# Routing by quarters, column-grouped logits and longer runs of slot work in an attention and mixture-of-experts kernel

## The chip, the cores and the metric

The kernel runs on one core of one Trainium2 chip. The metric is the device time of one execution in microseconds: before the change the median of 3 runs is 875.09 us (871.43 to 876.87). The profile is of one more execution, recorded by the hardware profiler; its span is 896.0 us. Five engines work side by side: TensorE (PE: matmuls and transposes; PEld is its weight load), VectorE (DVE), ScalarE (ACT), GpSimd (POOL) and SyncE (SP, which issues most transfers).

## The reference, cut to what matters

A sliding-window attention (8 batches, 8 heads, 576 positions, head width 64; four heads with a plain window of 32, four with a dilated one) makes 4608 rows of 512 numbers. Each row goes to one of 8 experts, chosen by the largest of 8 logits, and is multiplied by that expert's two matrices and by a gate.

```python
B, H, S, D = q.shape                      # 8, 8, 576, 64
scores = scale * np.matmul(q, k.transpose(0, 1, 3, 2))
...                                       # masks: window 32, or dilated by 4
attn = np.exp(scores); attn = attn / (np.sum(attn, -1, keepdims=True) + 1e-09)
x = np.matmul(attn, v)                    # then (B,H,S,D) -> (B*S, H*D) = (4608, 512)

logits = x @ w_gate                       # (4608, 8)
expert_idx = np.argmax(logits, axis=1)
probs = np.exp(logits - logits.max(-1, keepdims=True))
probs /= probs.sum(-1, keepdims=True) + 1e-09
gate_w = probs[np.arange(N), expert_idx]
...                                       # rows sorted by expert
h = np.maximum(x_sorted[lo:hi] @ w1[e], 0.0)      # w1[e]: 512 x 1024
y_sorted[lo:hi] = h @ w2[e]                       # w2[e]: 1024 x 512
return gate_w[:, None] * y                        # rows in their old order
```

All data is fp32.

## The kernel before

One Python program emits the instructions of three jobs, and a small clock in it decides how they are interleaved. A scheduler orders them within each engine.

**The attention** goes through 32 units (a batch has four: two kinds of window, two pairs of heads). Each unit turns q and k (`turned`), makes the scores in 64x64 pieces of the array (`scores`), the softmax (DVE, ACT, POOL), turns the weights (`weights`, two units later) and multiplies by v in 64-column pieces (`xo`). Its result is a quarter of `xT`, the batch's rows with the 512 features on the partitions. `yield` hands over to the other jobs with an estimate of cost.

```python
for i in range(len(units) + LAG):                       # LAG = 2
    if i >= LAG:
        eTs = weights(evs.pop(i - LAG))                 # 9 transposes, DVE copies
        yield 0.8, None
    if i < len(units):
        evs[i], dens[i] = front(qT["q"], qT["k"], units[i][1])   # 18 scores matmuls, softmax
    if 0 < i <= len(units):
        norm(evs[i - 1], dens.pop(i - 1))
    yield 1.7, None
    ...                                                 # turn q, turn k: yield 1.0 each
    if i >= LAG:
        for part in range(2):
            summed(eTs, b2, xTs[b2], ty2, hl2, part)    # 8 to 10 xo matmuls, an ACT copy to xT
            ...
            yield 0.9, (b2, xTs.pop(b2)) if last else None
```

**The routing** of a batch starts when all four quarters of its `xT` (128 x 4 x 576) are there. It turns the rows back (`xrow`), makes the logits, finds the expert, ranks the rows within each expert, and writes them to the expert's bucket in DRAM. After batches 1 to 7 it also makes the tables that say which expert and which bucket rows each slot takes.

```python
def route(b, xT):
    rows = []
    for i in range(NT):                                 # 6 tiles of TT = 96 rows
        ps = bank("xrow")
        for c in range(4):
            nc.tensor.transpose(ps[0:TT, 128*c : 128*c+128], xT[:, c, TT*i : TT*i+TT], ident)
        row = pool.tile([TT, ROW], F32, tag="row", name="row", bufs=6)
        (nc.vector.tensor_copy if i % 2 else nc.scalar.copy)(row[:, 0:DM], ps[0:TT])
        rows.append(row)
        yield
    ps = bank("logits")
    lg = ps[0:TT, 0 : NT * E].rearrange("p (t e) -> p t e", e=E)
    for i in range(NT):
        for c in range(4):                              # 24 matmuls, 8 columns wide
            nc.tensor.matmul(lg[:, i], lhsT=xT[:, c, TT*i : TT*i+TT], rhs=wg[:, c],
                             start=c == 0, stop=c == 3)
        ...
    nc.vector.tensor_reduce(out=top, in_=lg, axis=AX, op=OP.max)
    ...                                                 # one-hot of the first maximum, exp
    nc.vector.tensor_copy(before[:, 0], counts)
    for i in range(NT):
        nc.vector.tensor_tensor(out=before[:, i + 1], in0=before[:, i], in1=oh[:, i], op=OP.add)
    nc.vector.tensor_copy(counts, before[:, NT])
    yield
    ...                                                 # rank: 2 matmuls; gate; idx
    for i in range(NT):
        nc.vector.tensor_copy(rows[i][:, DM : DM + 1], gate[:, i : i + 1])
        nc.vector.tensor_scalar(rows[i][:, DM + 1 : ROW], const("tok", TT)[:, i : i + 1],
                                float(b * S), None, op0=OP.add)
        to_bucket(idx[:, i : i + 1], rows[i], b)        # indirect DMA from POOL's queue
    ...                                                 # yield; tables(s): some 30 small DVE operations
```

**The slots** are the experts' matmuls. A slot takes 128 rows of one expert: four transposes (`xt`), 32 matmuls with w1 (`ph`, in groups of four), and 8 with w2 of 512 columns (`py`). Each group of four `ph`, each `py` and each group of transposes is one piece of the slot generator. Only slots whose rows are already in the buckets may run during the attention (2, 6, 11, 15, 20 and 24 slots after batches 1 to 6). 39 slots run in all.

**The clock** owes slot work in proportion to attention work, and pays it at once, two times an attention step:

```python
ATT, BEHIND = 36.0, 16.0
def run_slots():
    while clock["owed"] > 0:
        while ready and ready[0][0] <= clock["all"]:
            _, upto, over = ready.pop(0)
            clock["upto"] = upto
            clock["rate"] = (SLOT * upto - clock["moe"]) / over
        ...                                             # stop at the last slot that is ready
        c = next(slots)                                 # one piece
        ...
        clock["owed"] -= c

for cost, ended in attention():
    clock["all"] += cost
    clock["owed"] += cost * clock["rate"] / 2 + 1e-6
    run_slots()
    if ended:
        routing.append((ended[0], route(*ended)))
    run_routing()                                       # one step of a routing
    clock["owed"] += cost * clock["rate"] / 2
    run_slots()
```

PSUM has 8 banks, which all matmul results take in turn (`bank`).

Of the kernel before, what the change touches and what calls it, by code (L numbers as in the profile page):

```python
# [29 lines left out]
ROW = DM + 2  # L30
# [14 lines left out]
def _constants():  # L45
# [10 lines left out]
    def mask(ty):  # L56
# [15 lines left out]
        "edge": np.tile(128 * np.arange(N // 128 + 1), (128, 1)),  # L72
# [23 lines left out]
def kernel(  # L96
# [17 lines left out]
    psum = ctx.enter_context(tc.tile_pool(name="psum", bufs=8, space=PSUM))  # L114
# [3 lines left out]
    wg = cpool.tile([128, 4, E], F32, name="wg")  # L118
    nc.scalar.dma_start(wg, moe_w_gate.rearrange("(c p) e -> p c e", p=128))
    counts = cpool.tile([96, E], F32, name="counts")  # L120
    nc.vector.memset(counts, 0.0)
# [201 lines left out]
    def summed(eTs, b, xT, ty, hl, part):  # L323
# [16 lines left out]
        if ty == 0:  # L340
# [5 lines left out]
            nc.scalar.copy(xT[:, hl, 64 * j0 : 64 * j1], xo[:, 0:n])  # L346
        else:
            for j in range(4):
# [5 lines left out]
                xT[:, 2 + hl].rearrange("p (t m a) -> p a m t", m=2, a=2)[:, part],  # L354
# [3 lines left out]
    def attention():  # L358
# [7 lines left out]
        xTs, evs, dens = {}, {}, {}  # L366
        for i in range(len(units) + LAG):
            if i >= LAG:
                eTs = weights(evs.pop(i - LAG))
                yield 0.8, None  # L370
# [4 lines left out]
            yield 1.7, None  # L375
# [8 lines left out]
            if i >= LAG:  # L384
                b2, ty2, hl2 = units[i - LAG]
                if (ty2, hl2) == (0, 0):
                    xTs[b2] = pool.tile([128, 4, S], F32, tag="xT", name=f"xT_{b2}")
                for part in range(2):
                    summed(eTs, b2, xTs[b2], ty2, hl2, part)
                    if part == 1 and hl2 == 1 and b2 + 1 < B:  # L390
                        load_v(b2 + 1, ty2)
                    last = (ty2, hl2, part) == (1, 1, 1)
                    yield 0.9, (b2, xTs.pop(b2)) if last else None

    def route(b, xT):


        rows = []
        for i in range(NT):
            ps = bank("xrow")  # L400
            for c in range(4):
                nc.tensor.transpose(  # L402
                    ps[0:TT, 128 * c : 128 * c + 128], xT[:, c, TT * i : TT * i + TT], ident
                )
            row = pool.tile([TT, ROW], F32, tag="row", name="row", bufs=6)
            (nc.vector.tensor_copy if i % 2 else nc.scalar.copy)(row[:, 0:DM], ps[0:TT])
            rows.append(row)
            yield
        ps = bank("logits")
        lg = ps[0:TT, 0 : NT * E].rearrange("p (t e) -> p t e", e=E)  # L410
        for i in range(NT):
            for c in range(4):
                nc.tensor.matmul(  # L413
                    lg[:, i],
                    lhsT=xT[:, c, TT * i : TT * i + TT],
                    rhs=wg[:, c],
                    start=c == 0,
                    stop=c == 3,
                )
            if i == 2:  # L420
                yield
# [12 lines left out]
        top, best = small("top", NT), small("best", NT)  # L434
        oh, dl, gate = small("oh", NT, E), small("dl", NT, E), small("gate", NT)
        nc.vector.tensor_reduce(out=top, in_=lg, axis=AX, op=OP.max)
        nc.vector.tensor_tensor(out=dl, in0=lg, in1=wide(top), op=OP.subtract)

        nc.vector.tensor_scalar(oh, dl, 0.0, None, op0=OP.is_ge)
        nc.vector.tensor_tensor(out=oh, in0=oh, in1=rev, op=OP.mult)  # L440
# [6 lines left out]
        before = small("before", NT + 1, E)  # L447
        nc.vector.tensor_copy(before[:, 0], counts)
        for i in range(NT):
            nc.vector.tensor_tensor(out=before[:, i + 1], in0=before[:, i], in1=oh[:, i], op=OP.add)  # L450
        nc.vector.tensor_copy(counts, before[:, NT])
# [398 lines left out]
```

## Time and profile before

| | busy us | share of the span | instructions |
|---|---|---|---|
| PE (matmul records) | 820.0 | 92% | 7006 |
| PEld (weight loads) | 633.1 | 71% | 7006 |
| DVE | 327.4 | 37% | 1057 |
| ACT | 204.7 | 23% | 751 |
| POOL | 143.3 | 16% | 131 |

The page cuts the span into 40 slices of 22.4 us; a digit is the busy share of a slice in tenths. PEclk is the granted TensorE clock in tenths of full speed. The table of groups names line, engine, operation, output<-inputs, shape and count, then the busy time, the mean ns of one, and the idle time before them with what ended it. An fp32 matmul appears as two records, a transpose as one. Matmuls are pipelined, so the mean of one is its latency; what it costs the queue is seen from start to start in the timeline.

### The profile page before, as it was taken

Reading aid. Unit: us, or ns where it says so; the run is one execution under the profiler, and the core shown is the slowest. Engines: PE = TensorE matmul, PEld = TensorE weight load, DVE = VectorE, ACT = ScalarE, POOL = GpSimd, SP = SyncE. Lnnn points to the kernel's source line nnn. Section 1 sums busy time; section 2 is a strip of 40 time slices with the busy share of each in tenths; the row PEclk is TensorE's granted clock in tenths of the full one; section 3 lists DMA queues with packets and bytes.
Section 4 is the critical chain, followed back from the end, with each engine's and each line's share of the span. In section 5 each row is a group of like instructions: output and inputs, shape, how many; then the busy total and the mean of one; then the engine's idle time right before and its main releaser. Section 6 shows DMA issues by size and latency. Waiting matters only on the chain.

```text
span 896.0 us, 18185 instructions
## 1 busy us (share of the span) xinstructions
PE 820.0 (92%) x7006; PEld 633.1 (71%) x7006; DVE 327.4 (37%) x1057; ACT 204.7 (23%) x751; POOL 143.3 (16%) x131
## 2 busy tenths in 40 slices
PE   4796978799999999999999989979999999999991
PEld 3685857677777777777777867847777676867770
DVE  4776667654643373344533441231010001101010
ACT  2562526143133222222223212100001010100000
POOL 0213132311311131113111120060000000000000
PEclk9896859889999999999999999989999999999996
DMA  9964638997999769988236546779931291549574
GB/s 196 179 149 111 132 85 305 261 249 232 326 263 309 256 180 263 293 254 284 69 118 190 189 152 228 270 233 336 322 120 48 85 308 59 209 143 322 211 250 179
DMA packets 145578, 187.46 MB, mean 209 GB/s; under 512 B 72206, under 2 KB 86030, under 8 KB 145488
## 3 DMA queue, kind: packets, MB, share of 16 engines
q1 hardware_dynamic: 137984, 165.74, 61.2%
q0 software_dynamic: 6832, 19.71, 6.3%
q8 instruction: 58, 0.95, 0.5%
q10 hardware_dynamic: 672, 0.79, 0.3%
q14 instruction: 32, 0.26, 0.1%
HBM read 216.58 MB, written 22.07 MB: 266 GB/s over the span
## 4 chain that ended last, share of the span: by engine, by line
PE 46%; issue 38%; DVE 5%; POOL 4%; DMA 2%; SPq 1%; another core or an unknown queue 1%; ACT 1%; POOLq 0%; DVEq 0%
PE ph L707 13%; PE py L731 13%; PE xo L332 4%; PE scores L269 3%; PE logits L413 3%; PE weights L317 3%; POOL out_dram L740 2%; PE xrow L402 2%; PE turned L242 2%; PE turned L234 1%; DMA k<-in_k_dram 1%; POOL bucket L157 1%; DVE e L280 1%; DMA w<-in_moe_w_dram 1%; DVE lo L289 1%
## 5 line engine op out<-in xcount | busy, mean ns | idle before, releaser
L707 PE MATMUL ph<-xt,w 128*128 128x128 f32 x2496 | 308.0, 277 | 6.3 <-issue 5.5
L707 PEld LDWEIGHTS ph<-xt,w 128*128 128x128 f32 x2496 | 293.5, 192 | 24.1 <-issue 20.9
L731 PE MATMUL py<-w,h 128*128 128x512 f32 x624 | 293.6, 608 | 6.7 <-DVE h L725 6.7
L731 PEld LDWEIGHTS py<-w,h 128*128 128x128 f32 x624 | 112.3, 193 | 112.5 <-issue 102.3
L292 ACT ACTIVATE e<-e,lo 128x96 f32<-128x96 f32 x288 | 103.6, 362 | 81.2 <-DVE lo L289 73.2
L740 POOL DMA_INDIRECT out_dram<-y,to x39 | 38.5, 986 | 401.5 <-ACT y L735 375.9
L683 DVE COPY xt<-xt 128x512 f32<-128x512 f32 x40 | 27.6, 689 | 191.9 <-PE xt L681 191.8
L307 POOL TENSOR_TENSOR e<-e,rec 128x864 f32<-128x864 f32 x32 | 52.2, 1631 | 236.7 <-DVE rec L306 147.7
L735 ACT ACTIVATE y<-py,x 128x512 f32<-128x512 f32 x39 | 26.7, 686 | 258.1 <-PE py L731 155.8
L319 DVE COPY eT<-weights 96x384 f32<-96x384 f32 x96 | 47.8, 546 | 90.1 <-PE weights L317 83.2
L725 DVE TENSOR_SCALAR h<-ph 128x512 f32<-128x512 f32 x39 | 26.9, 691 | 98.4 <-PE ph L707 86.6
L332 PEld LDWEIGHTS xo<-eT,v 96*64 96x64 f32 x1216 | 44.9, 149 | 22.4 <-issue 16.5
L157 POOL DMA_INDIRECT bucket<-row,idx x48 | 44.7, 930 | 95.1 <-DVE idx L481 31.0
L280 DVE SCALAR_TENSOR_TENSOR e<-scores,cst 128x384 f32<-128x384 f32 (+1 forms) x128 | 47.0, 399 | 27.8 <-PE scores L269 23.4
L332 PE MATMUL xo<-eT,v 96*64 96x64 f32 (+1 forms) x1216 | 52.7, 237 | 4.4 <-issue 4.4
L292 ACT ACTIVATION_READ_ACCUMULATOR e<-e,lo 128x1 f32 x288 | 53.9, 187 | 0.0
L317 PE MATMUL weights<-cst,e 128*96 128x128 f32 x288 | 44.2, 306 | 7.3 <-POOL e L307 6.4
L269 PE MATMUL scores<-kT,qT 64*64 64x96 f32 x1152 | 43.1, 284 | 8.1 <-DVE kT L239 4.5
L269 PEld LDWEIGHTS scores<-kT,qT 64*64 64x64 f32 x1152 | 35.2, 159 | 20.4 <-issue 9.9
L317 PEld LDWEIGHTS weights<-cst,e 128*96 128x96 f32 x288 | 36.7, 143 | 13.2 <-POOL e L307 8.2
L717 ACT ACTIVATE h<-ph 128x512 f32<-128x512 f32 x39 | 23.2, 596 | 97.9 <-PE ph L707 97.3
L353 ACT COPY xT<-xo 128x288 f32<-128x288 f32 x32 | 21.3, 680 | 82.0 <-PE xo L332 71.4
(103 smaller groups left out, 530.9 us busy)
## 6 DMA issues: line engine op xcount, KB each, us to landing
w<-in_moe_w_dram SPq DMA_DIRECT2D x82, 2048.0 KB
x<-bucket SPq DMA_DIRECT2D x41, 257.0 KB
v<-in_v_dram SPq DMA_DIRECT2D x32, 192.0 KB
q<-in_q_dram SPq DMA_DIRECT2D x32, 144.0 KB
k<-in_k_dram SPq DMA_DIRECT2D x32, 144.0 KB
v<-in_v_dram SPq DMA_DIRECT2D x48, 96.0 KB
q<-in_q_dram SPq DMA_DIRECT2D x8, 576.0 KB
k<-in_k_dram SPq DMA_DIRECT2D x8, 576.0 KB
```

What stands on the lines that cost most here:

```text
L157: nc.gpsimd.indirect_dma_start(out=bucket, out_offset=bass.IndirectOffsetOnAxis(ap=idx, axis=0), in_=rows, in_offset=None, bounds_check=NR ...
L269: nc.tensor.matmul(sc[r][64 * c : 64 * c + 64, 96 * (i % 5) : 96 * (i % 5) + 96], lhsT=qT[rows, 64 * j : 64 * j + 64], rhs=kT[rows, first_ ...
L280: nc.vector.scalar_tensor_tensor(out=e[p0:p1, i : i + n].rearrange("p i k -> p (i k)"), in0=sc[r][p0:p1, cols], scalar=-SCALE, in1=const(f ...
L292: nc.scalar.activation(out=e[:, n], in_=e[:, n], func=AF.Exp, bias=lo[:, n : n + 1], scale=-1.0, accum_out=den[:, n : n + 1],)
L307: nc.gpsimd.tensor_tensor(out=e, in0=e, in1=rec.unsqueeze(2).broadcast_to([128, 9, 96]), op=OP.mult)
L317: nc.tensor.transpose(tp[0:96, 128 * i : 128 * i + 128], e[:, a + i], ident)
L319: nc.vector.tensor_copy(eT, tp[0:96, 0:384])
L332: nc.tensor.matmul(xo[DH * h : DH * h + DH, at0 : at0 + nq], lhsT=vt[:, 2 * hl + r, j, :] if ty == 0 else vt[:, hl, j, DH * r : DH * r + D ...
L683: nc.vector.tensor_copy(xt, ps)
L707: nc.tensor.matmul(ph[:, fi], lhsT=w1[:, c, 128 * f : 128 * f + 128], rhs=xt[:, c], start=c == 0, stop=c == 3,)
L731: nc.tensor.matmul(py, lhsT=h[:, f], rhs=w2[:, f], start=f == 0, stop=f == 7)
L740: i = nc.gpsimd.indirect_dma_start(out=out, out_offset=bass.IndirectOffsetOnAxis(ap=to, axis=0), in_=y, in_offset=None, bounds_check=N - 1 ...
```

## The change

It is meant to make the routing cheaper and less of a lump, and to leave the slots' matmuls in longer runs.

1. After each attention unit, its quarter of `xT` (now a tile of its own, 128 x 576) is turned into rows at once, and its share of the logits is added up in a PSUM bank kept for that. The logits are computed the other way round: the gate's weights, padded to 32 columns, are the stationary operand and 192 rows of `xT` the moving one, three of them side by side in three column groups. Two transposes per batch (`lg`) turn the logits back. The rotating banks are 7.
2. The rows of a batch are one tile; the row number is written by one POOL operation, the gate by the reciprocal itself, and the counters are kept in one long tile.
3. The count of blocks in the tables is made with a shift in place of a comparison with a list; the tables are made in eight portions.
4. Slot work is paid only when at least 3.5 is owed (some four pieces).

```diff
-    psum = ctx.enter_context(tc.tile_pool(name="psum", bufs=8, space=PSUM))
+    psum = ctx.enter_context(tc.tile_pool(name="psum", bufs=7, space=PSUM))
+    lpsum = ctx.enter_context(tc.tile_pool(name="lpsum", bufs=1, space=PSUM))
...
+            if i > LAG:
+                b2, ty2, hl2 = units[i - LAG - 1]
+                row_part(b2, 2 * ty2 + hl2, xT)
+                yield 0.9, b2 if (ty2, hl2) == (1, 1) else None
...
+    def row_part(b, c, xT):
+        if c == 0:
+            rows[b] = pool.tile([TT, NT, ROW], F32, tag="rows", name=f"rows_{b}")
+            logits[b] = lpsum.tile([96, 2 * TT], F32, tag="logits", name=f"logits_{b}")
+            nc.gpsimd.tensor_scalar(
+                rows[b][:, :, DM + 1], const("tok", TT), float(b * S), None, op0=OP.add)
+        for i in range(0, NT, 3):
+            ps = bank("xrow")
+            for n in range(3):
+                nc.tensor.transpose(ps[0:TT, 128*n : 128*n+128],
+                                    xT[:, TT*(i+n) : TT*(i+n)+TT], ident)
+            (nc.scalar.copy, nc.vector.tensor_copy)[i // 3](
+                rows[b][:, i : i + 3, 128 * c : 128 * c + 128],
+                ps[0:TT, 0:384].rearrange("p (t d) -> p t d", t=3))
+        for j in range(3):
+            nc.tensor.matmul(logits[b][32*j : 32*j+32], lhsT=wg[:, c],
+                             rhs=xT[:, 2*TT*j : 2*TT*j+2*TT], start=c == 0, stop=c == 3)
+
+    def route(b):
+        row = rows.pop(b)
+        lgs = pool.tile([96, 2 * TT], F32, tag="lgs", name="lgs", bufs=1)
+        nc.vector.tensor_copy(lgs, logits.pop(b))
+        ps = bank("lg")
+        for i in range(2):
+            nc.tensor.transpose(ps[0:TT, 96*i : 96*i+96], lgs[:, TT*i : TT*i+TT],
+                                ident[0:96, 0:96])
...
-        nc.vector.tensor_scalar(oh, dl, 0.0, None, op0=OP.is_ge)
-        nc.vector.tensor_tensor(out=oh, in0=oh, in1=rev, op=OP.mult)
+        nc.vector.scalar_tensor_tensor(
+            out=oh, in0=dl, scalar=0.0, in1=rev, op0=OP.is_ge, op1=OP.mult)
...
-        nc.vector.tensor_copy(before[:, 0], counts)
-        nc.vector.tensor_copy(counts, before[:, NT])
...
-        nc.vector.reciprocal(gate, gate)
+        nc.vector.reciprocal(row[:, :, DM], gate)
...
-            nc.vector.tensor_copy(rows[i][:, DM : DM + 1], gate[:, i : i + 1])
-            nc.vector.tensor_scalar(rows[i][:, DM + 1 : ROW], ...)
-            to_bucket(idx[:, i : i + 1], rows[i], b)
+            to_bucket(idx[:, i : i + 1], row[:, i], b)
...
-        nc.vector.tensor_tensor(out=over, ...  op=OP.is_gt if last else OP.is_ge)
-        nc.vector.tensor_reduce(out=ns, in_=over, axis=AX, op=OP.add)
+        nc.vector.tensor_scalar(cnti, tot[0:p], 127.0 if last else 0.0, None, op0=OP.add)
+        nc.vector.tensor_scalar(nsi, cnti, 7, None, op0=OP.logical_shift_right)
+        nc.vector.tensor_copy(ns, nsi)
...                                           # and seven more yields inside tables(s)
-    ATT, BEHIND = 36.0, 16.0
+    ATT, BEHIND = 32.0, 12.0
+    GRAIN = 3.5
...
+        if clock["owed"] < GRAIN:
+            return
         while clock["owed"] > 0:
```

The costs that the attention reports to the clock are adjusted too (1.1 for 0.8 and 1.7, 0.75 for 0.9).

## The prediction

> **What bounds the kernel now.** I read the page's slices first, then the busy time by stage, then the groups by line, and last the instruction order of one stretch. The slices say which engine is full, and when:
>
> ```profile
> PE   4796978799999999999999989979999999999991
> DVE  4776667654643373344533441231010001101010
> PEclk9896859889999999999999999989999999999996
> ```
>
> From slice 9 on TensorE has no idle tenth except around slices 24 to 26, and its clock is full. Before that (about 25 to 185 us) no engine is full: TensorE shows 6 to 9 tenths at a lowered clock and VectorE 6 to 7. The stage table puts numbers on it (columns: stretch and its length, busy us of PE, PEld, DVE, ACT, POOL, granted clock, DMA share, GB/s):
>
> ```profile
> 25.00:185.00 160.00, 130.85 (x1719) 113.13 (x1718) 113.50 (x373) 67.50 (x306) 41.46 (x33) 0.79 0.70 176
> 185.00:520.00 335.00, 330.96 (x3094) 255.18 (x3093) 149.52 (x487) 95.74 (x361) 61.56 (x54) 1.00 0.76 231
> 520.00:605.00 85.00, 76.08 (x517) 57.26 (x517) 25.78 (x109) 10.21 (x17) 20.00 (x21) 0.94 0.65 225
> 605.00:880.00 275.00, 272.38 (x1577) 199.33 (x1575) 28.05 (x55) 24.40 (x38) 18.47 (x19) 1.00 0.58 203
> ```
>
> So there are three regimes: an attention-only start in which PE and DVE wait for each other, a PE-bound mix (185 to 520), and a PE-bound tail of bare slots (605 to 880, 14.45 us a slot). In the last two, a microsecond taken off PE's queue is a microsecond of the span; nothing else counts there. Hence the question is what PE's queue costs, group by group:
>
> ```profile
> L413 PE MATMUL logits<-wg,xT 128*96 128x8 f32 x384 | 35.3, 230 | 0.0
> L402 PE MATMUL xrow<-cst,xT 128*96 128x128 f32 x192 | 30.6, 279 | 0.8 <-ACT xT L353 0.6
> L269 PE MATMUL scores<-kT,qT 64*64 64x96 f32 x1152 | 43.1, 284 | 8.1 <-DVE kT L239 4.5 <-issue 2.5 <-DVE base L608 0.6
> L332 PE MATMUL xo<-eT,v 96*64 96x64 f32 x1088 | 49.8, 240 | 3.5 <-issue 3.5
> ```
>
> A busy mean (230 ns for an 8-column matmul) is latency, not spacing. The spacing is read from the timeline of PE, by subtracting start times (columns: start, busy, engine, line, group):
>
> ```profile
> 289.98 1.06 PE L707 MATMUL ph<-xt,w 128*128 128x128 f32 x8
> 290.96 1.04 PE L269 MATMUL scores<-kT,qT 64*64 64x96 f32 x36
> 291.94 2.05 PE L707 MATMUL ph<-xt,w 128*128 128x128 f32 x16
> 293.82 0.60 PE L402 MATMUL xrow<-cst,xT 128*96 128x128 f32 x4
> 294.26 1.06 PE L707 MATMUL ph<-xt,w 128*128 128x128 f32 x8
> 295.15 1.02 PE L731 MATMUL py<-w,h 128*128 128x512 f32 x2
> ...
> 306.27 1.95 PE L707 MATMUL ph<-xt,w 128*128 128x128 f32 x16
> 308.15 0.69 PE L332 MATMUL xo<-eT,v 96*64 96x64 f32 x16
> 308.77 1.16 PE L707 MATMUL ph<-xt,w 128*128 128x128 f32 x8
> 309.76 2.13 PE L413 MATMUL logits<-wg,xT 128*96 128x8 f32 x24
> 311.75 0.63 PE L681 MATMUL xt<-cst,x 128*128 128x128 f32 x4
> ```
>
> Each fp32 matmul is two records, a transpose one. Undisturbed, 8 ph records take 295.15 - 294.26 = 0.89 us, 0.111 each; an xrow transpose is (294.26 - 293.82) / 4 = 0.11. Going from ph to xrow and back costs nothing. A visit to the packed array does: 289.98 to 293.82 is 3.84 us for 24 ph (2.67) and one scores group, so the visit is 1.17 us, although its 36 records, in sets of four that run together, need 9 x 0.083 = 0.75. The fixed toll is about 0.42 us a visit. The same sum for xo (306.27 to 309.76 = 3.49, less 24 ph = 2.67, leaves 0.82 for 16 records) gives, with the 20-record visits that take 0.11 longer (so about 0.026 a record), a toll of about 0.40. The old logits are 1.99 us for 24 records, 0.083 each, though only 8 columns wide.
>
> **What the Trainium skill says.** "TensorE: Matmul & The Clock Gate", Part 3 (Packing small matmuls), says matmuls on different 32-column groups run concurrently, with 2.38 times for three groups at 512 columns. This trace agrees in kind: 36 scores records of 96 columns in 0.75 us are four-fold overlap. "TensorEngine Tiling (Array Packing)", Key Properties, says that a change of tiling mode drains TensorE; the 0.4 us toll above is what this trace shows of it. The first page's Part 1 says the clock is halved when PE idles and returns after sustained work; the granted 0.79 of 25 to 185 us against 1.00 later agrees.
>
> **The change part by part.**
>
> 1. Logits. Removed: 384 records x 0.083 = 31.7 us of PE (plus about 0.08 us on each of 16 returns, 1.3). Added: 96 matmuls, 192 records of 192 columns, in 32 visits of six. From 128 columns in 0.111 us and 512 in 0.43 (four py groups' starts), 192 columns should need 0.165 (estimate). Three column groups together, two passes: 0.33 us. But each visit now pays a mode toll that the old, full-height logits did not; I take 0.42 as for scores. In the built order a few visits are split, 35 in all: 35 x 0.42 + 32 x 0.33 = 25.3. The transposes back (16 of 96 columns at 0.083, some 0.4 more for transitions) add 1.7. Sum: 33.0 - 25.3 - 1.7 = 6 us saved. The packing is a smaller gain than it looks, since over half of it goes into tolls.
>
> 2. Slot runs of at least four pieces. Counted in the built orders, runs of slot work fall from 157 to 71, but going in and out of transposes costs nothing, as shown. What counts is that the two halves of one xo are parted less often: xo visits fall from 53 to 47, scores stay at 32. 6 x 0.40 = 2.4 us, and some 20 saved re-entries from the 72- and 96-row q/k transposes at about 0.03 (read from the timeline in the same way), 0.6. Sum: 3 us. The name of the change promises more than this.
>
> 3. VectorE. Removed per batch: 12 one-column writes (48 at 142 and 140 ns over the run: 11.4 us), two counter copies (2.0 + 1.3), one of the two one-hot operations (about 1.5), and most of the 288-wide count of blocks (3.0 + 2.6 + 0.9, for three small operations). Added: a 96x192 copy (about 0.35) and row copies of 96x384 in place of 96x512 (32 x 0.55 against 24 x 0.68, +1.2). Net some 15 us of 327. After 185 us VectorE is at 45% and this is worth nothing. In the start it is about 2 us a batch for three batches, beside PE's share already counted in 1. ScalarE's copies stay equal.
>
> 4. Spread tables and rows. The old routing stood in one lump at a batch's end; now each unit does a quarter, and the tables come in eight portions. In the start this fills PE more evenly. Against it: the logits copy, lg, eleven small VectorE operations and rank now follow closely in PE's queue, and in the first three batches no slot work lies between. I expect up to 2.5 us of PE waiting at lg and 2 at rank per batch, where the old order lost 2.7, 3.5 and 1.3 us before rank. I book parts 3 and 4 together as -2 us, +-6.
>
> 5. Banks. Seven rotating PSUM banks instead of eight, and bursts of three attention steps without slot work between: an evacuation that was hidden can now show. I book +0 to +3 us, say +0.5.
>
> 6. The slot schedule's figures (32 and 12 for 36 and 16) move slots forward by half a slot to one slot against the attention; in a PE-bound stretch this only reorders. Slot 24 is the first that needs the last table; in the new order the table is emitted at slot 22, so it does not starve.
>
> Sum: -6 - 3 - 2 + 0.5 = -10.5, about 1.2%: 875 - 10.5 = 864.5, and I say 864.
>
> **The rivals.** (a) The three column groups do not overlap, because both passes of one matmul hold the queue. Then a visit is 0.42 + 0.99 = 1.41 us, 32 of them 45 us, and the logits cost 12 us more than now: about 882. Against it stands the overlap of scores, and of xo, whose 16 records of 64 columns take 0.42 us, about half of what they would need one after the other. (b) The start is bound by VectorE and the cold clock, and the lighter, evenly spread routing lifts both: with 160 us at 0.79 clock, 10% there is 16 us more, about 850. For it: 113.5 us of VectorE in 160, and eight cold stretches. Against it: the longer lg-rank sequence opens new PE gaps at exactly this place, each of which can cool the clock. (c) The bursts expose VectorE and bank waits in 185 to 520, where now 4 us of 335 are idle. Two microseconds for each of the 17 units there would be 34 us; half a microsecond eats the whole gain: about 873. For it: scores waits for a kT copy only 2.2 us of PE work earlier. Against it: slot work still separates most such pairs, and VectorE is less than half busy. (d) The tail's stall (589 to 597 us, PE waiting for h while the last table is made) could go or grow with the yields: -7 to +5 us.
>
> **Range and chances.** The sure part is small, 6 to 9 us; the start and the tail each scatter by as much. Eight in ten: 850 to 877. Faster by over 2% needs 857.6 or less, that is rival (b) or (d) in its good form: 0.27. Slower by over 2% (892.6) needs (a) and (c) together: 0.05. Within 2%: 0.68.
>
> **What would show it.** Logits groups on PE: start to start of the next group under 0.75 us, and the first full-array matmuls after it spaced wider, prove part 1; 1.2 us or more prove rival (a). PE's gaps over 1 us before lg and rank in the first three batches measure part 4; the busy share of 185 to 520 and waits on DVE there, rival (c); the granted clock of 25 to 185 and the end of the first slot (193.9 us now), rival (b). I am wrong in kind if the first slot ends more than 10 us earlier or later, or if the mixed stretch shows over 10 us of new idle time.

## The result, and the profile after

The changed kernel takes 849.46 us (median of 4 runs, 846.83 to 856.43); the kernel before, run beside it, 875.98 us (4 runs, 871.43 to 881.16). The ratio is 0.9708, with an interval of 0.9626 to 0.979: some 26 us less, where I had booked 10.5. That lies just under my range of 850 to 877, in the case to which I gave a chance of 0.27. The profiled run of the changed kernel is the fastest of the four, with a span of 845.1 us. Absolute times differ by over 3% from chip to chip (the last experiment shows it), so below only ratios to the kernel before in the same comparison are set against each other.

The slices of the changed kernel's page (21.1 us each; rows as before):

```profile
PE   4779797999999999999999999999999999999991
DVE  3788795645533453445333631421010101111110
PEclk9997797999999999999999999999999999999996
```

The reader is to see two things. Before the last slice the clock row has no 5 and no 6 any more, and it shows 9 from the eighth slice (148 us) on instead of the tenth (202 us); and VectorE's row is fuller in slices 3 to 6 (8, 8, 7, 9). The stage table answers to the one in the prediction (same stretches, same columns):

```profile
25.00:185.00 160.00, 137.09 (x1873) 111.51 (x1872) 120.09 (x360) 76.16 (x344) 45.55 (x39) 0.87 0.80 204
185.00:520.00 335.00, 332.78 (x3030) 250.07 (x3029) 142.97 (x445) 90.80 (x336) 63.62 (x59) 1.00 0.76 241
```

In these first 160 us TensorE now issues 1873 records instead of 1719 (although the logits of a batch are now half as many records), at a clock of 0.87 instead of 0.79. The mixed stretch is full, as it was: 332.8 of 335 us. The page's busy shares would not have told this: PE is "93%" busy in the kernel before as it ran again (first experiment) and in the changed one. The Trainium skill, page "Perfetto Trace Analysis", section "Identifying the Most-Contended Engine", calls matmul busy time a bad measure of how near a kernel is to its bound, because matmuls are pipelined; this pair of traces agrees.

So I counted differently. Each PE record gets the start-to-start spacing that it has undisturbed at full clock (ph 0.112 us, py 0.429, transposes of 128 columns 0.109, xo 0.026, scores 0.021, old logits 0.083, all read from these timelines; new logits 0.055, a third of the 0.165 that the prediction estimates for 192 columns). Their sum is PE's work. Elapsed time less the work done by then is what was lost to waits, half clock and mode tolls. In us, from the profiled runs of the kernel before (first experiment below) and of the changed one:

```
                        work   lost by 100   by 200   by 500   by 650   span
before                 739.4          56.7     94.7    114.0    117.3   875.5
changed                719.6          54.5     82.9    104.7    106.5   845.1
```

The difference of 30.4 us is 19.8 less work (the logits, 31.7 -> 10.6, plus 1.3 for `lg`), about 12 less lost before 200 us, and about 1 more lost after it. What is lost after 200 us includes the new tolls. It is more than the 26 us of the medians, since the shortest of four executions stands here against a single one of the kernel before. Both the work and the start are larger than I had them.

### The profile page after: what moved, and what is told of

The parts are those of the page before. It is cut to its first block, busy times and chain, and to the rows that moved or that the text cites. A ratio compares the mean times of both kernels' runs of the same rounds, so it can differ in the third digit from the quotient of the medians.

```text
span 845.1 us, 17762 instructions
## 1 busy us (share of the span) xinstructions
PE 787.1 (93%) x6830; PEld 595.2 (70%) x6830; DVE 314.8 (37%) x955; ACT 203.5 (24%) x759; POOL 145.2 (17%) x139
## 4 chain that ended last, share of the span: by engine, by line
PE 48%; issue 30%; DMA 7%; DVE 7%; POOL 3%; ACT 2%; SPq 1%; POOLq 0%; DVEq 0%; ACTq 0%
PE ph L735 15%; PE py L759 15%; PE xo L335 4%; DMA v<-in_v_dram 4%; PE weights L320 3%; PE scores L272 3%; PE xrow L414 2%; DMA x<-bucket 2%; POOL out_dram L768 2%; ACT e L295 2%; DVE e L283 1%; PE turned L237 1%; PE logits L424 1%; DVE lo L292 1%; PE turned L245 1%
## 5 line engine op out<-in xcount | busy, mean ns | idle before, releaser
L735 PEld LDWEIGHTS ph<-xt,w 128*128 128x128 f32 x2496 | 291.9, 193 | 19.8 <-issue 16.1
L735 PE MATMUL ph<-xt,w 128*128 128x128 f32 x2496 | 300.6, 277 | 0.8 <-DVE xt L711 0.8
L759 PE MATMUL py<-w,h 128*128 128x512 f32 x624 | 280.6, 596 | 0.0
L160 POOL DMA_INDIRECT bucket<-rows,idx x48 | 44.5, 928 | 40.8 <-DVE idx L513 21.1
L335 PEld LDWEIGHTS xo<-eT,v 96*64 96x64 f32 x1216 | 42.3, 145 | 11.5 <-issue 7.5
L335 PE MATMUL xo<-eT,v 96*64 96x64 f32 (+1 forms) x1216 | 48.6, 233 | 1.8 <-DMA v<-in_v_dram 1.7
L320 PEld LDWEIGHTS weights<-cst,e 128*96 128x96 f32 x288 | 33.7, 137 | 9.7 <-POOL e L310 4.7
L272 PEld LDWEIGHTS scores<-kT,qT 64*64 64x64 f32 x1152 | 31.2, 148 | 11.9 <-issue 4.3
L272 PE MATMUL scores<-kT,qT 64*64 64x96 f32 x1152 | 37.7, 269 | 2.0 <-DVE kT L242 1.7
L414 PE MATMUL xrow<-cst,xT 128*96 128x128 f32 x192 | 28.4, 284 | 8.1 <-ACT xT L356 6.9
```

What stands on the lines that cost most here:

```text
L160: nc.gpsimd.indirect_dma_start(out=bucket, out_offset=bass.IndirectOffsetOnAxis(ap=idx, axis=0), in_=rows, in_offset=None, bounds_check=NR ...
L272: nc.tensor.matmul(sc[r][64 * c : 64 * c + 64, 96 * (i % 5) : 96 * (i % 5) + 96], lhsT=qT[rows, 64 * j : 64 * j + 64], rhs=kT[rows, first_ ...
L320: nc.tensor.transpose(tp[0:96, 128 * i : 128 * i + 128], e[:, a + i], ident)
L335: nc.tensor.matmul(xo[DH * h : DH * h + DH, at0 : at0 + nq], lhsT=vt[:, 2 * hl + r, j, :] if ty == 0 else vt[:, hl, j, DH * r : DH * r + D ...
L414: nc.tensor.transpose(ps[0:TT, 128 * n : 128 * n + 128], xT[:, TT * (i + n) : TT * (i + n) + TT], ident,)
L735: nc.tensor.matmul(ph[:, fi], lhsT=w1[:, c, 128 * f : 128 * f + 128], rhs=xt[:, c], start=c == 0, stop=c == 3,)
```

## The experiments

Medians in us; "before" is the kernel before on the same chip in the same comparison. e7, e9 and e10 ran on a second chip, e11 on a third, and the others on one.

| label | what it is | median (runs) | before (runs) | ratio and interval |
|---|---|---|---|---|
| e0_before_again | kernel before | 877.32 (1) | 875.70 (27) | |
| e1_grain_only | before + longer slot runs | 880.84 (22) | 875.70 (27) | 1.006 [1.0037, 1.0083] |
| e2_no_grain | changed, slot work paid at once | 849.95 (7) | 875.70 (27) | 0.970 [0.9672, 0.9729] |
| e3_old_logits | changed, old logits in quarters | 854.03 (6) | 875.70 (27) | 0.9754 [0.9725, 0.9782] |
| e4_light_dve | before + lighter VectorE work | 870.59 (8) | 877.37 (13) | 0.9937 [0.9903, 0.997] |
| e5_lump | changed, rows and logits in a lump | 848.89 (6) | 877.37 (13) | 0.9682 [0.9651, 0.9713] |
| e6_tables_whole | changed, tables in one portion | 856.68 (6) | 877.37 (13) | 0.9687 [0.9631, 0.9743] |
| e7_old_pace | changed, old figures of the schedule | 852.36 (6) | 875.75 (27) | 0.9757 [0.9716, 0.9797] |
| e8_warm2 | changed + filler matmuls in the start | 849.08 (6) | 877.37 (13) | 0.9674 [0.964, 0.9708] |
| e9_lump_old_logits | e5 and e3 together | 855.92 (6) | 875.75 (27) | 0.981 [0.9765, 0.9854] |
| e10_warm_before | before + filler matmuls in the start | 875.53 (22) | 875.75 (27) | 1.0008 [0.9985, 1.003] |
| e11_after_again | changed, on another chip | 882.12 (6) | 904.74 (11) | 0.976 [0.9714, 0.9805] |

No experiment leaves out any of the computation; the results of the filler matmuls in e8 and e10 go unused.

**The kernel before, once more.** The span of the first profile, 896.0 us, lies well above the median of 875, so I took another of the unchanged kernel.

> The kernel before, unchanged, for a second profile. Its first profile was of an execution 2.5% longer than the median. If the stalls of that profile (PE waiting 7 us at 589 us, three gaps of 1.3 us at 519 us, the first slot ending at 193.9 us) belong to the program, they stand here again and the span is near 896 us; if they belong to that one execution, the span is near 876 us and they are gone. The first slot's end then tells how much of the gain of the change lies in the start: theory 'start' (evenly spread routing lets the attention-only stretch run faster) expects the first slot to end at least 12 us later here than the 170.5 us of the changed kernel; theory 'queue' (PE's queue got shorter in the mixed stretch) expects under 6 us.

Its span is 875.5 us. The windows of this run (columns: stretch, length, busy us of PE, PEld, DVE, ACT, POOL, clock, DMA share, GB/s):

```profile
25.00:150.00 125.00, 103.57 (x1414) 92.65 (x1413) 91.97 (x285) 57.36 (x257) 32.46 (x25) 0.73 0.61 148
150.00:200.00 50.00, 44.58 (x494) 36.48 (x493) 31.08 (x111) 18.70 (x82) 12.90 (x11) 0.90 1.01 276
200.00:500.00 300.00, 298.66 (x2778) 232.40 (x2776) 133.44 (x425) 82.28 (x304) 52.08 (x46) 1.00 0.77 240
500.00:830.00 330.00, 330.00 (x2068) 243.50 (x2068) 56.31 (x199) 36.62 (x72) 42.09 (x43) 1.00 0.58 207
```

The same of the changed kernel:

```profile
25.00:150.00 125.00, 102.09 (x1480) 83.68 (x1482) 99.00 (x311) 61.85 (x281) 39.57 (x34) 0.84 0.77 197
150.00:200.00 50.00, 50.00 (x552) 38.55 (x547) 25.88 (x60) 18.22 (x76) 7.80 (x7) 0.99 0.95 264
200.00:500.00 300.00, 297.78 (x2720) 224.05 (x2719) 134.04 (x427) 83.87 (x320) 60.74 (x56) 1.00 0.75 235
```

The stall of the tail (76.08 of 85 us busy in 520 to 605 in the first profile) is not there: 330.00 of 330. My rival (d) was built on it. Whether it came from that one execution or from the chip it ran on isn't known; e11's profile has a stall of its own at 579 to 588 us. This trace is the "before" of what follows. The comparison also shows where the change works: up to 200 us. Up to 150 us PE is busy as long as before (103.6 and 102.1 us), with 66 records more, and VectorE is busier, not less: 99.0 of 125 us instead of 92.0. But the attention is no further by then: both have issued the scores of 15 units, and the loss as counted above is about 80 and 78 us. What differs is the first slot, whose matmuls begin at 132.5 us instead of 146.2, and with slot work at hand PE is busy 50.0 of the next 50 us at a clock of 0.99, instead of 44.6 at 0.90. About 10 of the 12 us come from there.

**Longer slot runs alone, and none.** In the kernel before I put the GRAIN rule alone (157 runs of slot work become 69, xo visits 53 -> 46); in the changed one I took it out (141 runs, 55 xo visits).

```diff
 e1, in the kernel before:            e2, in the changed kernel:
+    GRAIN = 3.5                     -    GRAIN = 3.5
+    if clock["owed"] < GRAIN:       -    if clock["owed"] < GRAIN:
+        return                      -        return
```

> The kernel before with only the rule that slot work is paid from 3.5 owed on. Slot runs fall from 157 to 69, xo visits from 53 to 46. My sum books 7 x 0.40 = 2.8 us plus 0.6 for q/k transposes: 872 to 873 us. A rival in which the runs themselves matter (each switch costs PE something that the start-to-start times do not show) expects 10 us or more: 866 or less. A rival in which bursts of attention expose evacuations expects 878 or more.

> The changed kernel with slot work paid at once as before (141 slot runs, 55 xo visits). By my sum it loses 8 x 0.40 + 0.6 = 4 us against the changed kernel: 853. If the gain is in the longer runs: 865 or more. If it is in the routing by quarters, in the start above all, 850 to 853.

Alone, the longer runs cost 0.6%. Without them the changed kernel keeps its ratio, 0.970. The saved visits are there in the order, but nothing of them reaches the time. In e1's profile 6 us more than in e0 are lost by 550 us (123.4 against 117.0), with 24 us more at half clock. It isn't rival (c), attention steps that wait for each other, for PE waits no more than in e0. From 200 to 550 us, e1 and then e0:

```profile
200.00:550.00 350.00, 349.15 (x3169) 272.11 (x3168) 148.88 (x504) 93.95 (x345) 62.77 (x55) 0.97 0.73 229
200.00:550.00 350.00, 348.66 (x3186) 268.71 (x3185) 150.49 (x503) 93.66 (x336) 62.38 (x56) 1.00 0.73 232
```

PE is as busy, but 20 us of this stretch are at half clock, and none in e0. Why the clock falls there stays open. The change's last-named part is the one that brings nothing.

**The old logits within the new routing.**

```diff
-        for j in range(3):
-            nc.tensor.matmul(logits[b][32*j : 32*j+32], lhsT=wg[:, c],
-                             rhs=xT[:, 2*TT*j : 2*TT*j+2*TT], ...)
+        for i in range(NT):
+            nc.tensor.matmul(logits[b][:, E*i : E*i+E], lhsT=xT[:, TT*i : TT*i+TT],
+                             rhs=wg[:, c, 0:E], ...)
```

The copy `lgs` and the transposes `lg` go as well.

> The changed kernel with the logits of each quarter as before: 96 rows of xT as the stationary operand, 8 columns moving, six tiles a quarter, and no transposing back; everything else as changed. By my sum PE's queue is 6 us longer in all: 855 to 856. If the packed logits cost as much as they save (toll of 0.42 us a visit and more), 849 to 851. If the packing is what brought the gain: 862 or more.

The ratio is 0.9754 instead of 0.9708, with intervals that overlap; against the variants of the changed kernel on the same chip that keep the packed logits and have tighter intervals (e2, e5 and e8; 0.970, 0.968 and 0.967) it is 0.5 to 0.8% slower. The changed kernel's own second ratio (e11, 0.976, on another chip) is no better than e3's, so the size of this gain stays rough. What a packed visit costs is seen in the changed kernel's timeline of PE (start, busy, engine, line, group):

```profile
304.74 1.95 PE L735 MATMUL ph<-xt,w 128*128 128x128 f32 x16
306.53 0.82 PE L414 MATMUL xrow<-cst,xT 128*96 128x128 f32 x6
307.28 0.53 PE L424 MATMUL logits<-xT,wg 128*32 128x192 f32 x6
307.74 0.71 PE L237 MATMUL turned<-cst,q 96*128 96x96 f32 x6
308.29 1.98 PE L735 MATMUL ph<-xt,w 128*128 128x128 f32 x16
310.10 3.60 PE L759 MATMUL py<-w,h 128*128 128x512 f32 x8
```

and in the tile's own view for that stretch (durations in ns, then first and last start):

```profile
L424 PE MATMUL logits<-xT,wg x6: 326/338/351, 307.3 to 307.5; 128*32 128x192 f32 x6
```

All six records start within 0.2 us and each lasts 0.34: three groups run at once, in two passes. From 306.53 to 310.10 there are 3.57 us. Take off 16 ph (1.79), six xrow (0.65) and six `turned` (0.50): 0.63 remain, of which 0.33 is the two passes. The toll is 0.30 us here, if the two passes take the estimated 0.33. The same count over the 11 undisturbed visits of six records between 200 and 520 us gives 0.27 to 0.28 where `turned` follows at once and 0.31 to 0.38 where slot matmuls or transposes follow, against 0.40 to 0.42 for the scores visits of the same kernel. All groups of the logits in the changed kernel (from the groups by form: line, engine, operation, tiles, shape, count, busy us, mean ns, idle before and its cause):

```profile
L414 PE MATMUL xrow<-cst,xT 128*96 128x128 f32 x192 | 28.4, 284 | 8.1 <-ACT xT L356 6.9 <-ACT xT L349 1.2
L424 PE MATMUL logits<-xT,wg 128*32 128x192 f32 x192 | 18.8, 346 | 0.8 <-ACT xT L356 0.8
L440 PE MATMUL lg<-cst,lgs 96*96 96x96 f32 x16 | 2.9, 266 | 3.8 <-DVE lgs L437 3.8
```

Given back by the packing: 3.8 us of waiting for the copy `lgs`, over 16 transposes. The 8.1 us before xrow belong to the quarters, not to the packing: the rows now follow directly on the copy of their quarter.

**VectorE's lighter work alone, in the kernel before.** One tile of rows, the row number by POOL, the reciprocal written into the row, a long counter tile, the merged one-hot, the shift. PE's instructions stay as they are, and their order but for four short moves.

```diff
-            nc.vector.tensor_copy(rows[i][:, DM : DM + 1], gate[:, i : i + 1])
-            nc.vector.tensor_scalar(rows[i][:, DM + 1 : ROW], ...)
+        nc.vector.reciprocal(row[:, :, DM], gate)
+        nc.gpsimd.tensor_scalar(row[:, :, DM + 1], const("tok", TT), float(b * S), ...)
...
-        nc.vector.tensor_copy(before[:, 0], counts)
-        nc.vector.tensor_copy(counts, before[:, NT])
...
```

> The kernel before with only the lighter small operations: one rows tile with the row number written by POOL and the gate by the reciprocal, the long counter tile, the merged one-hot operation, the count of blocks by a shift. Logits, the lump at the batch's end, the pace and the 8 banks stay as before. My sum put this at about 2 us a batch in the first three batches, 6 us at most: 870 to 874. If VectorE bounds the start and this lightening is where the gain is: 862 or less. If the start is set by something else: 874 to 877.

0.9937, which is 5.5 us, and in the profiles the loss up to 200 us falls by 6.5 (94.7 -> 88.2), and no further after. It is an effect of the start alone. Its window shows that it needs no emptier VectorE:

```profile
25.00:150.00 125.00, 104.63 (x1446) 93.82 (x1445) 90.92 (x258) 60.31 (x272) 32.98 (x27) 0.75 0.64 162
```

VectorE is as busy (90.9 us) with 27 instructions fewer, and PE is 32 records further at 150 us. I read this so: in this stretch VectorE's time is a supply, and what is taken off it is spent on the next unit. No run shows that step by itself.

**The lump.** The rows and logits of all four quarters are made at the batch's end again, one quarter a step; everything else stays as changed. This needs 8 tiles for xT and leaves one for the rows.

```diff
-                row_part(b2, 2 * ty2 + hl2, xT)
+                xTs.setdefault(b2, []).append(xT)
...
     def route(b):
+        for c, xT in enumerate(quarters.pop(b)):
+            row_part(b, c, xT)
+            yield
```

> The changed kernel with the quarters' rows and logits done together at the end of the batch, one quarter per step of the routing, as the lump stood before; packed logits, small operations, pace and runs as changed (the quarters wait in eight buffers, the rows have one). If the even spread is what shortens the start, 862 to 870, with the clock of 25 to 150 us falling back towards 0.73. If the spread is worth nothing, 849 to 853.

0.9682: no slower at all. I had expected a loss, so the even spread over the batch, the change's first-named part, isn't where the gain comes from. In its profile the loss by 200 us is 5 us above the changed kernel's, and some 2 us of that come back later; the medians show nothing of it.

**The tables in one portion.**

```diff
-                yield from tables(s)
+                for _ in tables(s):
+                    pass
```

> The changed kernel with the tables made in one portion as before. The slots become ready about one unit earlier by the clock of the program, so slot work starts about half a unit earlier; against it stand some 20 VectorE operations in one stretch. If the eight portions matter: 853 or more. If an earlier first slot is worth more: 846 or less. My sum has it at 849 +-2.

The six runs lie at 845.1, 854.7, 854.8 and three times at 858.6 to 859.0 us; the ratio of 0.9687 [0.9631, 0.9743] leaves out the last three, which count as slow, while the median in the table has all six. With them the result would fall in my "853 or more". No difference can be resolved in either direction.

**Filler matmuls in the changed kernel's start.** To see whether the clock itself limits the start, two constant matmuls of 480 columns per unit run until slots are due, about 20 us of PE's time.

```diff
+    def warm(n):
+        if clock["rate"] == 0.0:
+            for _ in range(n):
+                nc.tensor.matmul(bank("warm")[:, 0:480], lhsT=ident,
+                                 rhs=const("mask0"), start=True, stop=True)
```

> The changed kernel with two matmuls of 480 columns on constants added after each unit's scores and after each unit's logits, only until the first slots are due; their results are not used. They add about 0.8 us of PE each, 25 in all, some 20 us of PE work at full clock. If the half-speed stretches of the start (41 us of the changed kernel's first 151) cost time, and PE waits there anyway, the clock of 25 to 150 us rises from 0.84 to 0.95 or more and the time falls to 840 to 846. If the start is bound by VectorE and waits, and the clock does not matter, the time is 849 to 855. If the added work itself delays: 858 or more.

The clock of 25 to 150 us rises from 0.84 to 0.90 only (I had said 0.95), the time at half clock before 150 us falls from 40 to 27 us, and the ratio is 0.9674: some 20 us of filler neither lengthen nor shorten the time. What the same clock would do without the filler's own time on PE, no run shows.

**The old figures of the slot schedule.**

```diff
-    ATT, BEHIND = 32.0, 12.0
+    ATT, BEHIND = 36.0, 16.0
```

> The changed kernel with the schedule figures of before (36 and 16 for 32 and 12). Slots then stand about half to one slot later against the attention, 18 instead of 19 done when the last batch is routed. I booked nothing for this: 848 to 851. If moving slots forward fills PE's waits of the start, and part of the gain comes from it: 855 or more.

0.9757: about 4 us more than the changed kernel's first ratio, but the intervals overlap, and the changed kernel's second ratio (e11, 0.976) is the same as this one. So a cost isn't shown. In the profile the loss up to 200 us is 88.2 instead of 82.9. PE waits 5.0 us for a transfer of v at 139 us, where the changed kernel's longest such wait is 1.7, and by 150 us 15 us more have passed at half clock. Whether the old figures bring this wait isn't known: e3, with the new ones, has one of 4.0 us at 149 us. I had booked nothing for it.

**Lump and old logits together.** It has the work of the kernel before on PE (739.4 us), with neither the packing nor the spread.

> The changed kernel with both undone at once: the quarters in one lump at the batch's end, and the logits as before. Alone the lump cost nothing and the old logits 4.6 us. If the two parts simply add up, 853 to 855, and the clock of 25 to 150 us stays near 0.84. If the clock falls only where a lump and the thin old logits come together (some 4 us of 8-column matmuls and 2.6 us of transposes in a row, in which the array does little), the clock falls to about 0.75, over 60 us of the first 150 are at half speed, and the time is 861 or more.

0.981 [0.9765, 0.9854], against 0.9682 [0.9651, 0.9713] for the lump with the packed logits: here the packing is worth 1.3%, some 11 us, though the two ran on different chips. The clock of 0.81 and the 55 us of half clock before 150 us lie between my two cases, the median nearer to the additive one. Against e3 the intervals overlap. And it is still 1.9% under the kernel before, with neither of the change's first two names in it. The first stretch of e9, then e5, then e3:

```profile
25.00:150.00 125.00, 109.15 (x1584) 98.87 (x1582) 98.18 (x285) 61.66 (x276) 34.61 (x28) 0.81 0.73 191
```
```profile
25.00:150.00 125.00, 102.39 (x1513) 85.91 (x1511) 98.55 (x299) 64.53 (x293) 34.61 (x29) 0.86 0.75 189
```
```profile
25.00:150.00 125.00, 108.14 (x1490) 97.98 (x1488) 94.77 (x280) 61.37 (x278) 34.64 (x28) 0.84 0.68 180
```

All three have VectorE at 95 to 99 us of 125, above the 92 of the kernel before, whatever the form of the logits. What they share is the rest of the change. But it is no firm mark of the change: the changed kernel's second profile (e11) has 91.7.

**Filler matmuls in the kernel before.** This is the other half of the question about the clock: the same constant matmul, 24 times (48 records), in the start of the unchanged kernel.

> The kernel before with 24 matmuls of 480 columns on constants, until the first slots are due: one after each unit's scores, one after every second tile of rows, two in the logits; their results are not used. They add some 20 us of PE work at full clock. If the 75 us of half clock in the first 150 are what makes the start of the kernel before slow, the clock of 25 to 150 us rises from 0.73 to 0.85 or more and the time falls to 862 to 870 although there is more work. If the clock only follows from waits and costs nothing itself, the time is 874 to 880; if the added work delays, 882 or more.

```profile
25.00:150.00 125.00, 111.80 (x1526) 89.52 (x1525) 93.32 (x294) 61.00 (x276) 34.12 (x26) 0.91 0.64 170
150.00:200.00 50.00, 47.70 (x539) 37.27 (x539) 32.39 (x116) 17.30 (x74) 11.50 (x10) 1.00 0.91 238
200.00:225.00 25.00, 20.59 (x188) 19.43 (x189) 5.95 (x19) 4.42 (x16) 2.66 (x2) 0.80 0.87 297
```

The clock of the first stretch rises from 0.73 to 0.91, above the changed kernel's 0.84, and the time at half clock before 150 us falls from 75 to 24 us. By 200 us the kernel has done 12 us more of its own work than e0, the filler not counted. Yet the time is the same, 1.0008 [0.9985, 1.003]. In its profile two thirds of the gain are given back at once, in the third line above; 4 us are left at the end of this execution (871.4 against 875.5), and none in the medians. PE's timeline there, and what SyncE's queue waited for in that stretch (total us, times, longest):

```profile
207.29 0.69 PE L332 MATMUL xo<-eT,v 96*64 96x64 f32 x16
212.38 0.87 PE L694 MATMUL xt<-cst,x 128*128 128x128 f32 x3 [4.41 <-DMA x<-bucket]
```
```profile
SPq L213 <- DMA w<-in_moe_w_dram: 4.0, 1, 4.0
```

PE reaches a slot whose x isn't there: SyncE issued that load at 209.5 us, behind 13 loads of v, one of which had waited 4.0 us for a w transfer. The clock is at half from 210.6 us, within the wait of 4.4 us, to 220.8. In this profile a start made faster by filler ran into the next transfer.

**The changed kernel on another chip.**

> The changed kernel again, unchanged, for a second profile and a narrower interval than that of its four runs (0.963 to 0.979). If the gain is 2.9% the ratio stays within 0.968 to 0.973, and the undone versions can be set against it: the old logits cost 4 us or more only if this is 851 or less. Of its profile I expect what the first one showed: idle and half-clock time up to 200 us of 83 +-3 (kernel before: 95), 20 +-4 more from there to 600 us.

0.976 [0.9714, 0.9805] at 882.12 us against 904.74: the kernels take 3.8% and 3.3% longer there. The ratio is above the 0.968 to 0.973 that I had expected, though the interval overlaps that of the first, and the gain is 2.4 to 2.9%. The profile isn't what I had expected either:

```profile
25.00:150.00 125.00, 99.78 (x1421) 81.66 (x1419) 91.72 (x265) 61.38 (x279) 34.67 (x28) 0.84 0.67 177
150.00:200.00 50.00, 45.36 (x458) 35.67 (x457) 28.38 (x97) 15.25 (x66) 11.52 (x11) 0.86 0.95 238
```

By 200 us about 96 us are lost where I had said 83 +-3, and the first slot ends at 184.9 us instead of 170.5. No profile of the kernel before is known to come from this chip, so how much of the start's difference between e0 and the changed kernel holds on every chip stays open.

## Why the prediction was off

**Direction and mechanism of part 1 were right, the toll was mis-sized.** The overlap is shown (0.46 us from the first of the six records to the next group, where 1.2 was my mark for rival (a)), so rival (a) is false. The term "35 x 0.42" took the toll of another tile shape; the visits of 128x32 pay 0.27 to 0.38. With that the same sum is 35 x 0.27 (or 0.38) + 10.6 + 1.7 = 21.8 (or 25.6), and 7 to 11 us are saved instead of 6. The runs give 0.5% (e3) to 1.3% (e9 against e5), which is 4 to 11 us. The Trainium skill, "TensorEngine Tiling (Array Packing)", Key Properties, says that changing the mode drains TensorE; that a visit costs less in one shape than in another is in these traces only.

**Part 2 was right about the counts and wrong about the sum.** The runs and the xo visits fell as counted, but the 3 us for fewer xo visits did not appear either (e1 slower by 0.6%, e2 unchanged).

**Parts 3 and 4, "-2 us, +-6", is the step that failed, as far as the runs show.** I let the lighter VectorE work (2 us a batch for three batches, 6 in all) be eaten by new waits at lg and rank. The lighter work gives 5.5 us in the kernel before (e4), as worked out; over the whole span VectorE's busy time falls by 11 us (326.2 to 314.8) where I had some 15. The new waits came, but took the place of old ones. PE's waits from 25 to 150 us, before (e0; total us, times, longest):

```profile
PE weights L317 <- POOL e L307: 11.6, 4, 5.2
PE rank L455 <- DVE den L304: 3.1, 1, 3.1
PE rank L455 <- DVE oh L442: 2.5, 1, 2.5
PE scores L269 <- DVE base L608: 2.0, 1, 2.0
```

and changed:

```profile
PE xrow L414 <- ACT xT L356: 6.9, 5, 1.8
PE weights L320 <- POOL e L310: 4.0, 4, 2.5
PE lg L440 <- DVE lgs L437: 3.3, 2, 1.8
PE rank L487 <- DVE gate L501: 1.4, 1, 1.4
PE rank L487 <- DVE oh L474: 1.3, 2, 0.7
```

lg waits 3.3 us in all where I feared 2.5 a batch; the waits of rank shrink (before, they were 2.5, 3.1 and 1.0 us by the trace, a little less than the 2.7, 3.5 and 1.3 of the prediction). Against that stand 7.6 us fewer of waiting for the norm on POOL, which I had not seen at all. In all PE is idle no less than before in this stretch (21.4 us in e0, 22.9 changed). The 7.6 is not firm, for in the first profile of the kernel before the same wait is shorter:

```profile
PE weights L317 <- POOL e L307: 6.4, 3, 2.9
```

What such a wait is, in the kernel before (e0, all engines):

```profile
78.45 1.09 POOL L157 DMA_INDIRECT bucket<-row,idx  x1 [8.18 <-DVE idx L481]
79.84 0.92 POOL L157 DMA_INDIRECT bucket<-row,idx  x1 [0.30 <-issue]
...
82.92 0.20 DVE L306 RECIPROCAL rec<-den 128x9 f32<-128x9 f32 x1
83.51 0.92 POOL L157 DMA_INDIRECT bucket<-row,idx  x1 [0.30 <-DVE qT L239]
84.74 0.92 POOL L157 DMA_INDIRECT bucket<-row,idx  x1 [0.30 <-issue]
85.68 1.64 POOL L307 TENSOR_TENSOR e<-e,rec 128x864 f32<-128x864 f32 x1
87.38 0.88 PE L317 MATMUL weights<-cst,e 128*96 128x128 f32 x3 [5.15 <-POOL e L307]
```

The reciprocal is ready at 83.1 us, but in POOL's order the batch's six scatters, about 1.2 us each, come before the norm. It starts at 85.7, and PE idles 5.15 us. In e4 this wait is still there (12.7 us in the same stretch), so it is no part of those 5.5 us. With the lump put back (e5) it is 8.0 us, against 4.0 in the changed kernel; which edit moves it was not tried alone, and e5 was no slower for it.

**Part 6, booked as nothing, may be worth up to 4 us** (e7), in the start and not in the PE-bound stretch I looked at; the runs don't resolve it. **Part 5** was not tried alone; from 200 to 500 us 21.8 us are lost instead of 19.3, the new tolls included, so it can't have cost much.

**The rivals.** Rival (b) is the one that came: the start improved, and the first slot ends at 170.5 us instead of 191.6 (e0), well beyond the 10 us at which I called myself wrong in kind; with the old figures of the schedule it is 178.8 (e7), so some of that may be the earlier slots. But its reason was half right, and that its "about 850" fits is partly luck, since it had nothing of the packing's larger gain. A gain of the lighter VectorE is shown; the even spread (e5) is not the cause by itself, and filler that raises the clock (e8, e10) gains nothing. I read the granted clock of 0.79 as "10% there is 16 us more"; raising it by 25% with filler left the time where it was, and in the one profile of it two thirds of the gain went into the next transfer. Rival (c) is not seen: in the changed kernel the mixed stretch is as full as before (297.8 of 300 us), and in e1 too. Rival (d) took a stall that e0 lacks for one of the program.

**The account.** Of the 26 us: packing 4 to 11, lighter VectorE 5.5, pace 0 to 4, longer runs and spread nothing that shows, table portions not resolved. Some 6 to 16 us stay open, and the parts need not simply add. The open part lies in what e9 still has besides the lighter VectorE and the pace: three row tiles to a bank and a copy, xT as tiles of a quarter each, the new costs reported to the clock, and the new order of steps. I did not separate these.

## What to carry to other kernels

Put a price on a change of tiling mode from a timeline of that very mode: the toll was 0.42 us for one shape and 0.27 to 0.38 for another, and the estimate of the packing's gain went from 6 us to as much as 11 with it. In a start where several engines supplied each other and none was full, neither filler that raised the clock nor a smoother order was a gain by itself; 5.5 us came from taking work off the engine that supplies the others. Look also in the queues (POOL's scatters, SyncE's loads) for what stands before the thing that is waited for. Take a second profile of the kernel before when the first lies over its median, or stalls that the next one lacks enter the prediction.

## What was not expected of the hardware

- In the changed kernel the toll of a visit to the packed array, counted against estimated spacings, was 0.40 to 0.42 us for the 64x64 tiles of scores and 0.27 to 0.38 for the 128x32 tiles of the logits.
- Constant matmuls lifted the granted clock from 0.73 to 0.91, as the Trainium skill ("TensorE: Matmul & The Clock Gate", Part 1) lets one expect of sustained work; that 51 us less at half clock before 150 us, with some 20 us of filler, left the time where it was (1.0008) was not expected.
- Six indirect scatters in a row hold POOL's queue for some 7 us (0.92 us each and 0.30 between them), with a ready elementwise operation behind them.
- The same two programs took 3.3% (before) and 3.8% (changed) longer on another chip.
